# Unread TensorE products in the first stage's idle places, and the experts' ranks placed behind the one-hot tiles in the middle stage

## The chip, the cores and the metric

The kernel runs on one core of one Trainium2 chip. Times are device microseconds from the start to the end of one execution; a median is taken over three runs. The engines are TensorE (PE; its weight loads are listed as PEld), VectorE (DVE), ScalarE (ACT), GpSimd (POOL) and SyncE (SP). Each takes its own instructions in order; semaphores tie the engines together. SP issues most DMAs, POOL issues the ones that go through an index list.

## The reference

Attention over clusters, and on its output a mixture of eight experts of which each token uses two.

```python
mask = q_assign[:, :, :, None] == k_assign[:, :, None, :]
scores = scale * np.matmul(q, k.transpose(0, 1, 3, 2))
scores = np.where(mask, scores, -1000000000.0)
attn = np.exp(scores - max); attn = attn / (sum + 1e-09)
x = np.matmul(attn, v)                    # 4 x 768 tokens, 8 heads of 64 -> 3072 x 512
noisy_logits = x @ w_gate + np.log1p(np.exp(x @ w_noise)) * noise
top2 = np.argpartition(-noisy_logits, 2, axis=1)[:, :2]
h = np.maximum(x[mask] @ w1[e], 0.0)      # 512 -> 1024, for each expert e
out[mask] += top2_w[mask, k, None] * (h @ w2[e])
```

`q_assign` and `k_assign` are the nearest of 16 centroids. Batch 4, 8 heads, 768 positions, head size 64.

## The kernel before, in words

Attention runs over 16 pairs of heads, `p = 0..15`. For each pair 12 steps follow, one for each head of the pair and each block of 128 keys: `scores` multiplies keys with queries into two PSUM banks (`e0`, `e1`), ACT takes exp, POOL subtracts a bf16 half to leave a rest (`pl`), and `values` multiplies both halves with `v` into the bank `av`, four steps behind. Queries and keys stand in SBUF as f32 halves whose products are labelled f32 in the trace; the products with `v` and the transposes of one-hot rows (`identb`, `oh`, `gl`) are bf16 or f16. The largest score of each query is needed ahead of the exp: `b_max` (line 1049), for pair 0 `r_max` (line 1066), makes all scores once more and DVE reduces them (lines 1051, 1069). `r_max` works on half a block at a time; its products go to a ring of three banks, two for each half, and each is reduced from there.

A table of due steps (`AT`, `MOVE`) sets where in the loop each helper is issued. What stands ahead of step 0 is written out in the list `FIRST`: the load of the first queries, the clusters of pairs 0 and 1 (`a_sims`, line 952; `a_turn`, line 964; `a_max1`, `a_ge`, `a_ky`, `a_max2`, `a_eq` on DVE; `a_mask`, lines 1004 and 1015), and the first `r_max` calls. `b_negT` (line 1088) turns the largest scores.

Between attention and the experts lies the middle stage, whose order is the list `MID`: the gate of the last batch (`glog`, `glog2`, `gturn`, then `gate 0` to `gate 40`, where `gate 26` holds products on PE), the first layer of expert 0 on its first four tiles of tokens (`l1a 0..7`, line 1913, tile of F each, 512 columns), its second layer (`l2`, line 1954), the split of weights into two f16 halves (`spw1`, `spw2`, lines 1793 and 1795), and the loads of the next weights (`ldw1`, `ldw2`, lines 1870 and 1879). The list of expert 0's last tokens is made by `hot` (one-hot rows, DVE line 1408), `ent` (POOL lines 1418 and 1420), `lsum` (products on PE, line 1429) and `lend` (DVE line 1435, writes `idx`). With `idx` POOL gathers the rows of token tiles 4, 5, 6 (`gx 0 4..6`, line 1893), SP transposes them (`turn 0 4..6`, line 1904), and `l1b 0..7` runs the first layer on them. `rank 0` (DVE lines 1535 to 1541) orders experts 1 to 7 by load; SP reads its result `ids` into registers (line 1542), and only then can it issue `ldw1 1 0..3`, the four 512 KB loads of the next expert's `w1`. `rank 1` and `rank 2` (lines 1549, 1551) bring the lists into that order. All items of one engine keep the order of `MID`.

Of the kernel before, what the change touches and what calls it, by code (L numbers as in the profile page):

```python
# [9 lines left out]
F32 = mybir.dt.float32  # L10
# [24 lines left out]
    gate=7.667, gstep=[0.667, 0.167], am=5.333, amstep=0.333, cut=[13, 20], gplace=17.333,  # L35
# [244 lines left out]
}  # L280

FIRST = """fixed_init 1
c_turn
load_qk 0 0
a_hi 0 0
load_qk 0 1
a_sims 0
a_lo 0 0
constants2
load_qk 1  # L290
a_copy 0
a_turn 0
a_max1 0
a_ge 0
a_ky 0
# [16 lines left out]
r_max 0 1  # L312
r_max 0 0
a_turn 1
a_max1 1
p_hi 1 0
b_neg 0 0 1
# [13 lines left out]
a_max2 1""".splitlines()  # L331


MID = """turn 0 0
turn 0 1
turn 0 2
turn 0 3
gpg
spw1 0 0 1
spw1 0 1 1  # L340
spw1 0 2 1
spw1 0 3 1
ldw2 0 1
ldw2 0 2
ldw2 0 3
ldlist
mxw2 0 0
glog 0
glog 1
glog2 0  # L350
glog 2
glog2 1
glog 3
glog2 2
glog 4
glog2 3
glog 5
glog2 4
glog2 5
gturn  # L360
gate 0
gate 1
gate 2
gate 3
gate 4
# [5 lines left out]
gate 10  # L371
gate 11
gate 12
mxw2 0 1
l1a 0
xhi 13 0
xhi 13 1
xlo 13 0
xlo 13 1
xput 13  # L380
gate 13
gate 14
gate 15
gate 16
gate 17
gate 18
gate 19
l1a 1
xhi 14 0
xhi 14 1  # L390
xlo 14 0
xlo 14 1
xput 14
gate 20
gate 21
gate 22
gate 23
gate 24
gate 25
mxw2 0 2  # L400
l1a 2
xhi 15 0
xhi 15 1
xlo 15 0
xlo 15 1
xput 15
mxw2 0 3
l1a 3
gate 26
l1a 4  # L410
w2s 0 0
gate 27
gate 28
gate 29
gate 30
gate 31
l1a 5
w2s 0 1
gate 32
gate 33  # L420
gate 34
gate 35
spw2 0 0 0
spw2 0 0 1
l1a 6
spw2 0 1 0
spw2 0 1 1
l1a 7
spw2 0 2 0
spw2 0 2 1  # L430
spw2 0 3 0
spw2 0 3 1
eff 0 4
gate 36
gate 37
gate 38
gate 39
gate 40
l2 0
hot 0  # L440
ent 0 0
ent 0 1
hot 1
ent 1 0
ent 1 1
l2 1
lsum 0
lsum 1
lend 0
lend 1  # L450
eff 4 7
gx 0 4
gx 0 5
gx 0 6
rank 0
ldw1 1 0
ldw1 1 1
ldw1 1 2
ldw1 1 3
rank 1  # L460
rank 2
l2 2
count
mxw1 1 0
turn 0 4
turn 0 5
turn 0 6
gx 1 0
gx 1 1
gx 1 2  # L470
gx 1 3
l2 3
mxw1 1 1
mxw1 1 2
mxw1 1 3
l1b 0
l1b 1
w1s 1 0
l1b 2
w1s 1 1  # L480
turn 1 0
gx 1 4
l1b 3
turn 1 1
gx 1 5
l1b 4
ldw2 1 0
turn 1 2
gx 1 6
l1b 5  # L490
ldw2 1 1
mxw2 1 0
turn 1 3
l1b 6
ldw2 1 2
mxw2 1 1
l1b 7
pv
turn 1 4
l2 4  # L500
spw1 1 0 0
spw1 1 0 1
ldw2 1 3
mxw2 1 2
turn 1 5
turn 1 6
l2 5
spw1 1 1 0
spw1 1 1 1
spw1 1 2 0  # L510
spw1 1 2 1
spw1 1 3 0
spw1 1 3 1
mxw2 1 3
l2 6
ldcount""".splitlines()


def rap(tensor, offset, dims):
# [3 lines left out]
class Kernel:  # L523
# [128 lines left out]

    def psm(self):
        return self.bank("side")

    def rnorm(self, n, r):

        nc = self.nc
        nc.vector.tensor_scalar(n, n, 1e-37, None, op0=OP.max)
        nc.scalar.activation(r[:, 0:1], n, AF.Sqrt)  # L660
        nc.vector.reciprocal(r[:, 1:2], r[:, 0:1])
        nc.vector.scalar_tensor_tensor(n, n, r[:, 1:2], r[:, 0:1], op0=OP.mult, op1=OP.add)
        nc.vector.tensor_scalar(n, n, 0.5, 1e-6, op0=OP.mult, op1=OP.add)
        nc.vector.reciprocal(n, n)
# [23 lines left out]
    def attention(self, ctx):  # L688
        nc, tc = self.nc, self.tc
        B, H, S, D, NJ = self.B, self.H, self.S, self.D, self.NJ  # L690
# [132 lines left out]
        rank = {self.a_lo: -1, self.a_hi: 1}  # L823
        for t in range(min(sched)[0], z + L + 2):
            u = t - L
            slot = lambda i: [f(*a) for _, f, a in sorted(sched.pop((t, i), []), key=lambda x: x[0] + rank.get(x[1], 0) if t > -24 else 0)]
            slot(0)
            if 0 <= t < z:
                self.scores(t // 12, (t % 12) // 6, t % 6)
            if 0 <= t - 1 < z:  # L830
                self.split_p((t - 1) // 12, ((t - 1) % 12) // 6, (t - 1) % 6)
            slot(1)
            if 0 <= u < z:
                p, s, kc = u // 12, (u % 12) // 6, u % 6
                for i in range(NJ):
                    if AT["vd"][i] == kc:
                        self.values(p, s, i)
            slot(2)
        assert not sched

    def first(self, do):
        for f in FIRST:
            name, *a = f.split()
            by = [self.nc.scalar] if a[-1:] == ["ACT"] else []
            do(getattr(self, name), *(int(x) for x in a[:len(a) - len(by)]), *by)
# [207 lines left out]
    def r_max(self, p, j, half=None):  # L1053

        nc, st, NJ = self.nc, self.st[p], self.NJ
        hl, mk = st["hl"], st["mk"]
        if "mm" not in st:
            st["mm"] = self.wk.tile([128, 2 * NJ, 2], F32, name="mm")
        js = slice(j * 128, j * 128 + 128)
        for n in range(2) if half is None else (half,):  # L1060
            ns = slice(n * 384, n * 384 + 384)
            ts = [self.ps()[:, :384] for s in range(2)]
            for a, b, first in ((hl[:, 1], hl[:, 2], True), (mk[:, 0], mk[:, 1], False)):
                for s in range(2):
                    r = slice(64 * s, 64 * s + 64)
                    nc.tensor.matmul(ts[s], a[r, js], b[r, ns], start=first, stop=not first)
            for s in range(2):
                c = NJ * s + j if p else NJ * (j // 3) + 3 * s + j % 3
                nc.vector.tensor_reduce(st["mm"][:, c, n:n + 1], ts[s], axis=X, op=OP.max, negate=True)
# [65 lines left out]
    def values(self, p, s, kc):  # L1135
        nc, st, H, D, NJ = self.nc, self.st[p], self.H, self.D, self.NJ
        b, hp = divmod(p, H // 2)
        h = 2 * hp + s
        if kc == 0:
            st["av", s] = self.psum.tile([128, NJ, 65], F32, name="av", bufs=1)  # L1140
            if s == 0:
                if p < self.NP - 2:
                    self.xp[p] = self.gp.tile([128, NJ, 128], F32, name="xp", bufs=2)
                else:
                    t = self.mw.tile([128, self.F], F32, name="stg", bufs=7)
                    self.xp[p] = t[:, :NJ * 128].rearrange("p (j c) -> p j c", c=128)
        av = st["av", s]
        vv, am = self.vv[b, h // 4], self.am[b, h // 4]
        head = (lambda j: 2 * (hp % 2) + j // 3) if p in ROWS else (lambda j: h % 4)
        ph, pl = st.pop(("p", s, kc))  # L1150
        kj = 2 * (kc % 3) + kc // 3
        for j in range(NJ):
            js = slice(j * 128, j * 128 + 128)
            nc.tensor.matmul(av[:, j, :], ph[:, js], vv[:, head(j), kj, 64:129], start=(kc == 0 and j == 0),  # L1154
                             stop=False, skip_group_check=True)
            nc.tensor.matmul(av[:, j, :64], ph[:, js], vv[:, head(j), kj, 0:64], start=False,  # L1156
                             stop=False, skip_group_check=True)
        for j in range(NJ):
            js = slice(j * 128, j * 128 + 128)
            nc.tensor.matmul(av[:, j, :], pl[:, js], vv[:, head(j), kj, 64:129], start=False,  # L1160
                             stop=(kc == NJ - 1), skip_group_check=True)
        if kc == NJ - 1:
            rs = self.wk.tile([128, NJ], F32, name="rs")
            if p in ROWS:
                xo = self.xp[p].rearrange("p (m a) (s d) -> p a s m d", a=2, s=2)[:, s]
            else:
                xo = self.xp[p].rearrange("p (j a) c -> p a j c", a=2)[:, :, :, s * D:s * D + D]
            nc.vector.tensor_scalar(rs, av[:, :, 64], 64e-9, am[:, 0:1] if p else am[:, 2:3], op0=OP.add, op1=OP.mult)
            nc.vector.reciprocal(rs, rs)
            two = lambda x: x.rearrange("p (a j) d -> p a j d", a=2)  # L1170
            nc.vector.tensor_tensor(xo, two(av[:, :, 0:64]), two(rs[:, :, None].to_broadcast([128, NJ, D])), op=OP.mult)
# [424 lines left out]
    def experts(self, ctx):  # L1596
# [13 lines left out]
        self.fs = self.g_gate(b)  # L1610
        for item in MID:
            name, *a = item.split()
# [413 lines left out]
```

## Time and profile before

| what | us |
|---|---|
| median of 3 runs | 1004.48 (1002.84 to 1007.99) |
| the profiled execution, its own time | 1005.61 |
| its span, first to last instruction | 1003.8 |
| PE busy in it | 948.3 (94%) |
| DVE, POOL, ACT busy | 653.6, 565.9, 487.5 |
| mean granted TensorE clock | 0.976 |

A row of a timeline gives start, duration, engine, line, operation, output and inputs, how many instructions are merged in it, and in brackets the time that the engine stood idle ahead of it and what ended that. A row of a table by stretches gives busy time (and number of instructions) of each engine. The granted clock is a share of 2.4 GHz, so 0.50 is 1.2 GHz.

### The profile page before, as it was taken

Reading aid. Unit: us, or ns where it says so; the run is one execution under the profiler, and the core shown is the slowest. Engines: PE = TensorE matmul, PEld = TensorE weight load, DVE = VectorE, ACT = ScalarE, POOL = GpSimd, SP = SyncE. Lnnn points to the kernel's source line nnn. Section 1 sums busy time; section 2 is a strip of 40 time slices with the busy share of each in tenths; the row PEclk is TensorE's granted clock in tenths of the full one; section 3 lists DMA queues with packets and bytes.
Section 4 is the critical chain, followed back from the end, with each engine's and each line's share of the span. In section 5 each row is a group of like instructions: output and inputs, shape, how many; then the busy total and the mean of one; then the engine's idle time right before and its main releaser. Section 6 shows DMA issues by size and latency. Waiting matters only on the chain. (4 is left out here: it accounts for less than half of the span.)

```text
span 1003.8 us, 21267 instructions
## 1 busy us (share of the span) xinstructions
PE 948.3 (94%) x8063; PEld 609.8 (61%) x8063; DVE 653.6 (65%) x1406; ACT 487.5 (49%) x1081; POOL 565.9 (56%) x649
## 2 busy tenths in 40 slices
PE   5999999999989998789789999999999999999997
PEld 2567788887878887664455545445455455454553
DVE  6678788888878978856636555456555564565421
ACT  3567778786868684467042415306224153151420
POOL 9369898899999999912435225225243352342301
PEclk9599999999999999999989999999999999999999
DMA  5377999999989963071495925728529358294201
GB/s 176 94 174 187 207 239 208 241 207 246 209 195 215 220 138 109 11 163 49 154 196 148 247 98 127 231 87 210 184 68 263 117 120 231 81 233 142 81 11 51
DMA packets 146160, 159.72 MB, mean 159 GB/s; under 512 B 85213, under 2 KB 112093, under 8 KB 146054
## 3 DMA queue, kind: packets, MB, share of 16 engines
q1 hardware_dynamic: 132668, 120.95, 50.0%
q0 software_dynamic: 12864, 36.37, 11.6%
q10 hardware_dynamic: 522, 1.00, 0.5%
q8 instruction: 64, 1.05, 0.5%
q14 instruction: 42, 0.34, 0.1%
HBM read 77.30 MB, written 26.05 MB: 103 GB/s over the span
## 5 line engine op out<-in xcount | busy, mean ns | idle before, releaser
L1132 POOL TENSOR_TENSOR pl<-pe 128x768 f16<-128x768 f32 x173 | 250.9, 1467 | 28.2 <-ACT pe L1113 10.4
L1913 PEld LDWEIGHTS <-w1t 128*128 128x128 f16 x1536 | 149.9, 98 | 119.9 <-DMA xT<-xg 8.8
L1051 DVE TENSOR_REDUCE mm<-m 128x1 f32<-128x384 f32 x360 | 186.3, 550 | 24.5 <-PE m L1049 22.7
L1121 ACT ACTIVATE pe<-e 128x384 f32<-128x384 f32 x360 | 157.0, 489 | 90.0 <-PE e L1120 84.1
L1954 PEld LDWEIGHTS <-hT 128*128 128x128 f16 x1152 | 112.2, 98 | 133.9 <-issue 1.1
L1966 POOL DMA_INDIRECT out<-yo,idx x50 | 60.2, 1204 | 228.8 <-DVE yo L1962 103.3
L1913 PE MATMUL m<-xT,w1t 128*128 128x400 f16 (+4 forms) x756 | 163.0, 333 | 0.0
L1913 PE MATMUL e<-xT,w1t 128*128 128x400 f16 (+4 forms) x528 | 133.8, 338 | 8.6 <-DMA xT<-xg 8.0
L1119 PE MATMUL e<-A 128*128 128x384 f32 x360 | 131.4, 365 | 7.0 <-issue 2.7
L1789 DVE TENSOR_TENSOR hT<-hr,hT 128x384 f16<-128x384 f32 (+6 forms) x128 | 70.1, 557 | 88.0 <-ACT hT L1788 68.6
L1954 PE MATMUL m<-w2t,hT 128*128 128x512 f16 x576 | 127.0, 379 | 0.0
L1049 PE MATMUL m<-A 128*128 128x384 f32 x360 | 119.6, 382 | 5.7 <-DVE mm L1051 1.7
L1120 PE MATMUL e<-B 128*128 128x384 f32 x360 | 122.3, 340 | 0.0
L1154 PE MATMUL av<-vv,pe 128*128 128x65 f16 x1152 | 98.3, 196 | 0.0
L1156 PE MATMUL av<-vv,pe 128*128 128x64 f16 x1152 | 96.9, 193 | 0.0
L1893 POOL DMA_INDIRECT xg<-xs,idx x50 | 51.9, 1038 | 77.4 <-DMA xT<-xg 67.1
L1154 PEld LDWEIGHTS <-pe 128*128 128x128 bf16 x1152 | 76.7, 98 | 22.9 <-issue 18.7
L1786 ACT ACTIVATE hr<-m 128x400 f32<-128x400 f32 (+4 forms) x63 | 32.1, 509 | 117.1 <-PE m L1913 105.6
L1786 ACT ACTIVATE hr<-e 128x400 f32<-128x400 f32 (+4 forms) x44 | 22.5, 511 | 129.7 <-PE e L1913 92.3
L1954 PE MATMUL e<-w2t,hT 128*128 128x512 f16 x384 | 85.0, 379 | 0.0
L1049 PEld LDWEIGHTS m<-A 128*128 128x128 f32 x360 | 64.9, 192 | 24.8 <-DVE mm L1051 13.5
L1913 PE MATMUL side<-xT,w1t 128*128 128x400 f16 (+4 forms) x252 | 78.6, 334 | 0.0
(302 smaller groups left out, 1567.9 us busy)
## 6 DMA issues: line engine op xcount, KB each, us to landing
stg<-in_moe_w SPq DMA_DIRECT2D x64, 512.0 KB
qt<-in_qk SPq DMA_DIRECT2D x15, 768.0 KB
A<-hl SPq DMA_DIRECT2D x28, 384.0 KB
B<-hl SPq DMA_DIRECT2D x28, 384.0 KB
vt<-in_v SPq DMA_DIRECT2D x8, 768.0 KB
out<-zt SPq DMA_DIRECT2D x12, 512.0 KB
xs<-xh SPq DMA_DIRECT2D x15, 384.0 KB
A<-hl SPq DMA_DIRECT2D x56, 96.0 KB
```

The source lines that it names most:

```text
L1049: nc.tensor.matmul(t, A[:, s, 0, j * 128:j * 128 + 128], A[:, s, 1, n * 384:n * 384 + 384], start=True, stop=True)
L1051: nc.vector.tensor_reduce(st["mm"][:, self.NJ * s + j, n:n + 1], t, axis=X, op=OP.max, negate=True)
L1119: nc.tensor.matmul(t, A[:, s, 1, ks], A[:, s, 0, ns], start=True, stop=False)
L1120: nc.tensor.matmul(t, Bt[:, 0, s, ks], Bt[:, 1, s, ns], start=False, stop=True)
L1121: nc.scalar.activation(pe[:, n], t, AF.Exp, scale=self.scale)
L1132: (nc.vector if last else nc.gpsimd).tensor_tensor(lo, pe, hi, op=OP.subtract)
L1154: nc.tensor.matmul(av[:, j, :], ph[:, js], vv[:, head(j), kj, 64:129], start=(kc == 0 and j == 0), stop=False, skip_group_check=True)
L1156: nc.tensor.matmul(av[:, j, :64], ph[:, js], vv[:, head(j), kj, 0:64], start=False, stop=False, skip_group_check=True)
L1789: nc.vector.tensor_tensor(h1, r[:, a:b], h0, op=OP.subtract)
L1913: nc.tensor.matmul(p, self.w1t[:, wi, c, f * 128:f * 128 + 128], self.xT[e][:, c, xi, n0:n1], start=(i == 0), stop=(i == 3 * ND - 1))
L1954: nc.tensor.matmul(p, self.hT[:, hi, f, t * 128:t * 128 + 128], self.w2t[:, wi, f], start=(i == 0), stop=(i == 3 * NF - 1))
L1966: i = nc.gpsimd.indirect_dma_start(out=self.out, out_offset=bass.IndirectOffsetOnAxis(ap=en[:r], axis=0), in_=yo[:r], in_offset=None, boun ...
```

## The change

Two things are changed. The list `FIRST` and the function `r_max` get groups of products of the bf16 identity with itself, written to bank `e1`, which nothing reads: 10, 2, 2, 18 and 4 in `FIRST` and 2 in each half of `r_max` for blocks 0 to 4 (20), each 384 columns wide. In steps 11 and 12 eight more, 122 columns wide, go to the unused end of bank `av`, whose tile is now a whole bank. And the order of `MID` is rewritten.

```diff
 FIRST = """fixed_init 1
+warm 10
 c_turn
+warm 2
 load_qk 0 0
...
 a_lo 0 0
+warm 2
 constants2
...
 a_turn 0
+warm 18
 a_max1 0
...
 a_turn 1
+warm 4
 a_max1 1
...
+    def warm(self, n):
+        t = self.bank("e1")
+        for _ in range(n):
+            self.nc.tensor.matmul(t[:, :384], self.identb, self.identb[:, None, :].to_broadcast([128, 3, 128]), start=True, stop=True)
+    def warm_av(self, n):
+        for _ in range(n):
+            self.nc.tensor.matmul(self.avt[:, 390:512], self.identb, self.identb[:, :122], start=False, stop=False,
+                                  skip_group_check=True)
...
+            if t in (11, 12):
+                self.warm_av(8)
             if 0 <= t < z:
                 self.scores(t // 12, (t % 12) // 6, t % 6)
...
+            if j < NJ - 1:
+                self.warm(2)
             for s in range(2):
...
-            st["av", s] = self.psum.tile([128, NJ, 65], F32, name="av", bufs=1)
+            self.avt = self.bank("av")
+            st["av", s] = self.avt[:, :65 * NJ].rearrange("p (j c) -> p j c", c=65)
```

Of `MID`, the part after `l1a 3` now reads

```diff
+l1a 3
+gate 38
+gate 39
+hot 0
+mxw2 0 3
+xput 14
+hot 1
...
+rank 0
+ldw1 1 2
+ldw1 1 0
...
 l1a 7
+lsum 0
...
 lsum 1
 lend 0
```

The four rows of `r_max` products for one half are followed on PE at once by the next half's in the kernel before (output, then inputs; the number after a name tells buffers apart):

```order
L1066 MATMUL m_258<-A_117 128x384
L1066 MATMUL m_259<-A_117 128x384
L1066 MATMUL m_258<-B_120 128x384
L1066 MATMUL m_259<-B_120 128x384
L1066 MATMUL m_268<-A_117 128x384
L1066 MATMUL m_269<-A_117 128x384
L1066 MATMUL m_268<-B_120 128x384
L1066 MATMUL m_269<-B_120 128x384
```

and now, with the line numbers of the changed kernel:

```order
L1085 MATMUL m_297<-A_117 128x384
L1085 MATMUL m_298<-A_117 128x384
L1085 MATMUL m_297<-B_120 128x384
L1085 MATMUL m_298<-B_120 128x384
L665 LDWEIGHTS identb
L665 MATMUL e_303<-identb 128x384
L665 LDWEIGHTS identb
L665 MATMUL e_303<-identb 128x384
L1085 MATMUL m_310<-A_117 128x384
L1085 MATMUL m_311<-A_117 128x384
```

Two weight loads and two products on bank `e1` stand between the halves. In the middle stage DVE's order from the one-hot tiles to the ranks was, before:

```order
L1408 TENSOR_TENSOR hot<-aux,lower 128x768 x2
L1960 TENSOR_SCALAR yo<-m_9459,we 128x512
L1435 TENSOR_TENSOR idx<-m_9490,lst 128x56
L1437 TENSOR_TENSOR lsw<-m_9490,lst 128x56
L1862 TENSOR_SCALAR we<-lsw,ce 128x3
L1535 SCALAR_TENSOR_TENSOR rk<-base,num 128x8
L1536 TENSOR_TENSOR rg<-rk 128x49
L1537 TENSOR_REDUCE rk<-rg 128x7
L1538 TENSOR_TENSOR perm<-rk,num 128x49
L1539 TENSOR_TENSOR rg<-perm,num 128x49
L1541 TENSOR_REDUCE ids<-rg 128x7
```

and is now (`hT` is the rest half of a tile of the first layer):

```order
L1811 TENSOR_TENSOR hT<-hr,hT 128x512
L1409 TENSOR_TENSOR pk<-aux,pk 128x12
L1410 SCALAR_TENSOR_TENSOR rec<-aux,px,gm 128x6
L1430 TENSOR_TENSOR hot<-aux,lower 128x768 x2
L1811 TENSOR_TENSOR hT<-hr,hT 128x512
L1395 TENSOR_TENSOR base<-aux,base 128x8
L1829 TENSOR_REDUCE gmax<-m_9434 4x1
L1830 TENSOR_SCALAR gmax<-gmax 4x1
L1557 SCALAR_TENSOR_TENSOR rk<-base,num 128x8
L1558 TENSOR_TENSOR rg<-rk 128x49
L1559 TENSOR_REDUCE rk<-rg 128x7
```

The ranks no longer stand behind the second layer's output `yo` and the list `idx`; they follow the one-hot tiles with one `hT` between, and the one-hot tiles follow the fourth `hT` and not the eighth. On PE the products of `lsum` stood between the second and the third output tile of the second layer (line 1954 and 1976):

```order
L1954 LDWEIGHTS hT
L1954 MATMUL m_9459<-w2t,hT 128x512
L1429 MATMUL m_9490<-ent,hot 128x112 x12
L1954 LDWEIGHTS hT
L1954 MATMUL m_9563<-w2t,hT 128x512
```

Now they stand between the last hidden tile and the first output tile:

```order
L1935 LDWEIGHTS w1t
L1935 MATMUL e_9530<-xT,w1t 128x512
L1451 MATMUL side<-ent,hot 128x112 x12
L1976 LDWEIGHTS hT
L1976 MATMUL m_9586<-w2t,hT 128x512
```

The two output tiles that were ahead of `lsum` are behind it. In all PE has 144 rows more, a weight load and a product for each of the 72 unread products.

## Rows read from the trace of the kernel before

**Rows 1.** Busy time by stretches (from:to, length, each engine, granted clock, DMA share, GB/s)
```profile
0.00:17.00 17.00, 6.13 (x34) 2.63 (x36) 9.46 (x32) 7.46 (x13) 15.84 (x39) 1.00 0.41 148
17.00:20.50 3.50, 2.64 (x15) 1.46 (x14) 2.88 (x6) 0.34 (x1) 3.33 (x6) 0.99 0.96 264
20.50:31.20 10.70, 8.37 (x30) 5.13 (x30) 9.17 (x21) 1.55 (x2) 4.99 (x7) 0.50 0.65 142
31.20:51.20 20.00, 19.32 (x87) 12.57 (x85) 11.65 (x27) 12.01 (x26) 9.08 (x8) 0.50 0.32 90
...
450.40:496.60 46.20, 45.65 (x236) 22.17 (x234) 30.12 (x85) 19.23 (x37) 16.48 (x25) 1.00 0.27 80
496.60:504.60 8.00, 0.00 (x1) 0.00 (x0) 4.32 (x4) 0.00 (x0) 1.11 (x2) 0.82 0.97 270
504.60:520.80 16.20, 15.53 (x99) 10.42 (x100) 5.73 (x21) 5.80 (x21) 7.87 (x8) 0.88 1.06 221
```
**Rows 2.** Timeline of PE in the first stage
```profile
6.59 1.51 PE L952 MATMUL side<-qt,cb 128*32 128x384 f32 x8 [0.63 <-DVE cb L686]
8.71 0.90 PE L964 MATMUL side<-ident,sm 128*128 128x128 f32 x3 [0.61 <-ACT sm L958]
13.50 0.82 PE L1004 MATMUL side<-identb,gl 128*128 128x128 bf16 x6 [3.88 <-DVE gl L988]
...
15.22 1.51 PE L952 MATMUL side<-qt,cb 128*32 128x384 f32 x8 [0.26 <-ACT B L1009]
...
25.97 0.45 PE L1088 MATMUL m<-ident,nm 128*128 128x128 f32 x1 [1.29 <-DVE nm L1083]
```
**Rows 3.** Timeline of PE, the same operations later, at granted clock 1.00
```profile
55.16 0.49 PE L964 MATMUL side<-ident,sm 128*128 128x128 f32 x3
64.52 0.51 PE L1015 MATMUL side<-identb,oh 128*128 128x128 bf16 x6 [0.67 <-DVE oh L993]
70.79 0.85 PE L952 MATMUL side<-qt,cb 128*32 128x384 f32 x8
```
**Rows 4.** Timeline of DVE in the first stage
```profile
1.28 0.86 DVE L555 TENSOR_SCALAR identb<-lg 128x128 bf16<-128x128 f32 x1
12.88 0.56 DVE L988 TENSOR_TENSOR gl<-side,km 128x384 bf16<-128x384 f32 x1 [0.73 <-POOL gl L858]
17.47 3.22 DVE L1069 TENSOR_REDUCE mm<-m 128x1 f32<-128x384 f32 x6 [1.85 <-PE m L1066]
20.89 1.02 DVE L1069 TENSOR_REDUCE mm<-m 128x1 f32<-128x384 f32 x2 [0.19 <-PE m L1066]
22.23 1.02 DVE L1069 TENSOR_REDUCE mm<-m 128x1 f32<-128x384 f32 x2 [0.32 <-PE m L1066]
```
**Rows 5.** Timeline of PE after the middle stage's idle time
```profile
504.65 3.36 PE L1913 MATMUL e<-xT,w1t 128*128 128x320 f16 x12 [8.04 <-DMA xT<-xg]
507.80 2.17 PE L1913 MATMUL side<-xT,w1t 128*128 128x320 f16 x12
...
509.92 1.79 PE L1913 MATMUL m<-xT,w1t 128*128 128x320 f16 x12
512.33 0.38 PE L1814 MATMUL m<-gmax,fw 4*128 4x1 f32 x2 [0.62 <-DVE gmax L1808]
```
**Rows 6.** Timeline of SP's DMA issues
```profile
491.02 2.02 SPq L1870 DMA_DIRECT2D stg<-in_moe_w  x4
493.16 15.59 SPq L1904 DMA_TRANSPOSE xT<-xg  x5
```
**Rows 7.** Timelines of POOL and DVE around the lists of expert 0
```profile
486.77 1.04 POOL L1893 DMA_INDIRECT xg<-xs,idx  x1 [1.10 <-DVE lsw L1437]
...
487.99 0.20 DVE L1541 TENSOR_REDUCE ids<-rg 128x7 int32<-128x49 f32 x1
```
**Rows 8.** Timeline of PE in the middle stage
```profile
467.00 5.35 PE L1913 MATMUL e<-xT,w1t 128*128 128x512 f16 x24
...
483.74 2.51 PE L1429 MATMUL m<-ent,hot 128*128 128x112 f32 x21
```

More of the change, by code (lines that the diff above doesn't have):

```diff
@@ L331 @@
 a_max2 1""".splitlines()
-MID = """turn 0 0
+MID = """gpg
+spw1 0 0 1
+mxw2 0 0
+spw1 0 1 1
+turn 0 0
 turn 0 1
@@ L337 @@
 turn 0 3
[L338 to L341, printed above, removed]
+glog 0
+ldw2 0 1
+ldw2 0 3
 spw1 0 3 1
[L343 to L348, printed above, removed]
 glog 1
+glog 2
 glog2 0
-glog 2
 glog2 1
 glog 3
+spw1 0 2 1
 glog2 2
 glog 4
+glog 5
 glog2 3
-glog 5
 glog2 4
+ldlist
 glog2 5
@@ L362 @@
 gate 1
+ldw2 0 2
+xhi 13 0
 gate 2
@@ L373 @@
 gate 12
[L374 to L377, printed above, removed]
+gate 13
 xlo 13 0
-xlo 13 1
-xput 13
-gate 13
 gate 14
@@ L387 @@
 gate 19
-l1a 1
+gate 20
+gate 22
+gate 23
+gate 34
+gate 24
+gate 25
+l1a 2
+mxw2 0 1
+xhi 13 1
 xhi 14 0
 xhi 14 1
+gate 21
+l1a 0
+xlo 13 1
+l1a 1
+mxw2 0 2
 xlo 14 0
+gate 26
+gate 28
 xlo 14 1
[L393 to L401, printed above, removed]
-xhi 15 0
[L403 to L414, printed above, removed]
+xput 13
+xhi 15 0
 gate 30
 gate 31
+xhi 15 1
+gate 33
+gate 37
+gate 27
+xlo 15 0
+gate 36
+xlo 15 1
+gate 40
+gate 32
+gate 35
+l1a 3
[5 more added lines that the diff above has]
+hot 1
+ent 0 0
+xput 15
+l1a 4
+gate 29
+w2s 0 0
+ent 1 0
+rank 0
+ldw1 1 2
+ldw1 1 0
+ent 1 1
 l1a 5
+ent 0 1
+ldw1 1 1
+ldw1 1 3
 w2s 0 1
[L419 to L422, printed above, removed]
 spw2 0 0 0
@@ L426 @@
 spw2 0 1 0
-spw2 0 1 1
 l1a 7
+lsum 0
 spw2 0 2 0
[L430 to L447, printed above, removed]
 lsum 1
 lend 0
-lend 1
-eff 4 7
+spw2 0 3 0
 gx 0 4
 gx 0 5
-gx 0 6
[L455 to L459, printed above, removed]
-rank 1
[L461 to L467, printed above, removed]
+turn 0 4
+eff 0 4
+spw2 0 1 1
+turn 0 5
+lend 1
+gx 0 6
+turn 0 6
+spw2 0 2 1
+spw2 0 3 1
+mxw1 1 0
+l2 0
+l2 1
+mxw1 1 1
+mxw1 1 3
+mxw1 1 2
+l2 2
+w1s 1 0
+rank 2
+rank 1
+gx 1 1
 gx 1 0
-gx 1 1
+gx 1 4
 gx 1 2
-gx 1 3
-l2 3
-mxw1 1 1
-mxw1 1 2
-mxw1 1 3
+eff 4 7
+ldw2 1 1
+l2 3
+w1s 1 1
+ldw2 1 0
+mxw2 1 0
+turn 1 0
+gx 1 5
 l1b 0
 l1b 1
-w1s 1 0
 l1b 2
-w1s 1 1
-turn 1 0
-gx 1 4
 l1b 3
+gx 1 6
+l1b 4
+l1b 5
 turn 1 1
-gx 1 5
-l1b 4
-ldw2 1 0
+l1b 6
 turn 1 2
[L489 to L496, printed above, removed]
 l1b 7
-pv
-turn 1 4
-l2 4
 spw1 1 0 0
 spw1 1 0 1
-ldw2 1 3
-mxw2 1 2
-turn 1 5
[L506 to L514, printed above, removed]
-l2 6
-ldcount""".splitlines()
+spw1 1 2 0
+spw1 1 3 0
+spw1 1 1 0
+spw1 1 2 1
+spw1 1 1 1
+count
+ldw2 1 2
+gx 1 3
+spw1 1 3 1
+mxw2 1 2
+l2 4
+ldw2 1 3
+turn 1 3
+mxw2 1 1
+l2 5
+pv
+mxw2 1 3
+turn 1 4
+turn 1 5
+l2 6
+ldcount
+turn 1 6""".splitlines()
 def rap(tensor, offset, dims):
```

## The prediction, made before the changed kernel ran

> **What bounds the kernel now.** I read the table of stretches first [rows 1]: it tells in which stages PE is not the whole of the time, and at which of its two levels the clock stands there. From 450 us on PE is busy nearly throughout, but for one hole: 8.00 us from 496.6 with no product. In the first stage it is idle 10.9 of the first 17 us, and from 20.5 to 51.2 it works at 0.50, that is 1.2 GHz; from 31.2 it is busy 19.32 of 20.00 us and still at 0.50. Next I read PE's timeline there [rows 2]. The table says clock 1.00 for the first 17 us, but the durations say otherwise: three transposes take 0.90 us at 8.71 and 0.49 us later, six one-hot transposes 0.82 against 0.51, the eight sims products 1.51 against 0.85 [rows 2, 3]. I take the durations: half clock up to about 16.7 us, full to 20.5, half again to 51.2. Third, DVE's timeline [rows 4]: the reduces of the first six run back to back (3.22 us for six); with the clock down, each pair of them waits for PE. Last the hole [rows 5 to 7]: PE waits for the transposes of expert 0's last three token tiles, SP issues them at 493.16 behind four loads of `w1` (491.02), those wait for `ids` (487.99), and the gather itself starts at 486.77.
>
> So two places can give time: the half clock of the first stage, and the hole with the slow products behind it. Elsewhere PE's own work is the time, and the change leaves it alone.
>
> **The first stage, part by part.** A product of 384 columns is not in the trace. Twelve of 320 take 3.36 us at half clock and 1.79 at full [rows 5]; by columns that makes 0.32 us and 0.16 us (an estimate from these rows). The 72 added products are 56 of these, 9 us at full clock or 18 at half, and 16 of 122 columns, under 1 us.
>
> The first 10 can start when `identb` is there, at 2.14 us [rows 4], and take 3.2 us at half clock: done at 5.4, when ScalarE's centroids come (the sims products follow at 6.59). The next two pairs lie in gaps of 0.63 and 0.61 us [rows 2], which they fill: cost 0 to 0.1 us each. The 18 behind the transposes at 8.71 lie in a gap of 3.88 us [rows 2]: 2.9 us at full clock, hidden, 5.8 at half, of which 1.9 stick out. I take full clock, since in the trace a burst of transposes and sims products from 13.50 to 16.7 was followed by it, and here 3 us of products and the sims stand ahead.
>
> Gain at the start: DVE's `gl` cannot be earlier, it waits for POOL (12.88) [rows 4]. Behind it the two times six transposes and the sims products shrink by 0.31 and 0.66 us on the path, some 1.1 us with ScalarE between; bounds 0 and 1.3.
>
> Gain in `r_max`: DVE is busy 9.17 of 10.70 us there [rows 1]. Its waits of 0.19 and four times 0.32 us [rows 4] go at full clock: 1.5 us. The two products added for each half take 0.33 us, in the time in which PE waits for DVE's reduce (a pair of reduces is 1.02 us, PE's four products some 0.5). Cost 0 at full clock. At half clock they take 0.64 us of a half that PE already sets; ten halves then lose some 0.3 us each, 3 us. The group of 4 lies in a gap of 1.29 us [rows 2].
>
> Then the scores, 20.00 us at half clock [rows 1], from step 0 to the first product with `v`. No unread products stand there. Will the clock hold? Before it fell at 20.5, PE had done only f32 products since 16.7; and 19 us of f32 products on a busy PE did not bring it back [rows 1]. In contrast the f16 products at 504.65 were at full clock after 3.2 us [rows 5]. So in this kernel f32 products do not seem to hold it. The last bf16 product is the one-hot transposes behind step 0; I let the full clock last some 4 us past them, as it did from 16.7. Some 5 us of work at full clock replace 7 at half: 2 us. Later the products with `v` begin at half clock, which costs 0.5 us that before did not. First stage: 1.1 + 1.5 + 2 - 0.5 = 4.1 us.
>
> If the clock held throughout, the 20 us would shrink to about 14 (ScalarE alone has 12.01 us of work there, DVE 11.65 [rows 1]): 1.1 + 1.5 + 6 = 8.6 us, less what waits anew; say 8. The rest of attention follows in the same order and PE-bound, so what is gained by then stays.
>
> The Trainium skill ("TensorE: Matmul & The Clock Gate", section "Why this matters for your kernels") asks only for a TensorE kept busy without long gaps to have the full clock. By that rule the unread products hold it and the busy scores keep it: 8 us instead of 4.1. The rows speak against it: busy 19.32 of 20.00 us, clock 0.50 [rows 1]. The same page (section "Terms") puts the loss at the throttled time times one minus the clock's share. By that, 30.7 us at half would give back 15.4 us. The rows put ScalarE and DVE in the way, 12.01 and 11.65 us in the 20, 9.17 in the 10.7 [rows 1]; I keep 4.1.
>
> **The middle stage.** Now `lsum` follows the last hidden tile, which ended at 467.00 + 5.35 = 472.3 us [rows 8]. Its one-hot tiles and entries must be there by then. PE's place products come after three hidden tiles instead of four; behind them DVE has the small gate operations, one `hT` and the two one-hot tiles, about 6 us, and POOL's eight entries end some 2 us later: about 468, an estimate with 4 us to spare. So `lsum` ends at 472.3 + 2.5 = 474.8, and `idx` is there 11.5 us before its present place: the gather moves from 486.77 to about 475.3 [rows 7]. The `ids` come about 469 instead of 487.99, and the four loads about 472 instead of 491 [rows 6]. Those loads lie beside expert 0's first and second layers, in a stretch with a DMA share of 0.27 [rows 1]. The three transposes then land before 490, while PE's work for `l2 0..3` still ends near 496.6: its sum is unchanged, `lsum` only moves. The hole of 8.04 us goes [rows 5].
>
> With no hole the clock does not fall: the first twelve products of `l1b` take 1.79 instead of 3.36 us, the next 1.79 instead of 2.17, and the wait of 0.62 for `gmax` goes, because the scale of the next `w1` stands ahead of `l1b` now [rows 5]. Together 8.04 + 1.57 + 0.38 + 0.62 = 10.6 us.
>
> What is late next: expert 1's inputs. Its first product would come at about 523. Its seven gathers and transposes start when `rank 1` is done, behind the third output tile: 474.8 + 3 x 5.2 = 490.4 [rows 8], and some 4 us of DVE work, say 495. Five transposes took 15.59 us beside loads [rows 6], 3.1 us each; seven take 22, and two loads of `w2` (the four of `w1` held the queue some 9 us, so 2.3 each) another 4.6. That is 26.4 of 28 us. The last transposes also stand behind the register load of the overflow count. I take 0.7 us of loss; bounds 0 and 6 (4 us for each transpose, with share 1.06 [rows 1]).
>
> The sum against the profiled execution's own 1005.61 us: 4.1 + 10.6 - 0.7 = 14.0, so 991.6. That execution stands 1.1 us above the median of 1004.48; against the median 990.5.
>
> **Rivals.** A: the clock holds through the first stage (for it: the rule above; against: the rows named there): 8 + 10 = 18 us, 986.5. B: the unread products do not hold the clock in `r_max`, being a minority beside f32 work. Then 1.1 us are gained at the start and the 3 us of the ten halves lost; with 9.9 us of the middle stage, about 996. That the products change nothing in the clock at all belongs here. C: the hole is only moved to expert 1's start: 4.1 + 10.6 - 6 leaves 8.7, so 996. D, slower: the 56 products run at half clock and none is hidden, 18 us, because they sit ahead of the operations that PE is waited for. It decides from 34 of the 56 exposed (10.6 us): 1004.48 + 18 - 10.6 = 1012. Against it: gaps of 0.61 to 3.88 us are measured at most places.
>
> **How the numbers follow.** Forecast 0.48 (its own range 988 to 993.5), A 0.18, B 0.15, C 0.13, D 0.06. The unknown costs (start 0 to 1.3, the unread products in `r_max` 0 to 3, expert 1 0 to 6) take the range to 984.5 below, into A, and 998 above, over B and C. Half a per cent is 5 us, about what this kernel's measurement can tell from no change (three runs spread over 5.15 us). Above 999.5 lie the tail of B and C with both losses (0.06) and D: faster 0.89, same 0.06, slower 0.05.
>
> **What would show it.** Full clock from about 7 us, one-hot transposes in 0.5 us, `r_max` reduces without waits, clock falling again some 5 us into the scores (not at all: A; before `r_max`: B). In the middle: loads of `w1` issued near 472, `lsum` right behind the hidden tiles, no wait for `xT` ahead of `l1b`, its first twelve products in 1.8 us, expert 1 starting near 523 less the first stage's gain. A PE wait there for `xT` is C. I am wrong if the end of `l2 3` is late, because the hidden tiles wait for DVE's gate operations ahead of them.

## The result, and the profile after

| | us, median | runs |
|---|---|---|
| before | 1004.7 (1000.4 to 1017.9) | 18 |
| after | 992.39 (990.3 to 1001.0) | 18 |
| ratio | 0.9874, 95% interval 0.9855 to 0.9893 | |
| forecast | 990.5 (984.5 to 998.0) | |

The change brings 12.7 us (1004.7 x 0.0126; by the interval 10.8 to 14.6). The forecast had 14.0. The profiled execution took 992.97 us, its span 991.2.

Kernels are compared only with the kernel before on the same chip, since the chips differ: its medians there were 1004.7, 1007.5 and 996.5, and single runs took 994.4 and 996.0 us. In one execution each of two kernels the time was 5317 us, and the one profile of these shows TensorE at a sixth of its rate (24 products of 512 columns take 32.09 us, in the changed kernel 5.34); they enter no median or ratio of this text, and the repeat of the changed kernel below has no other profile.

The table of stretches of the changed kernel, in the form of [rows 1] (length, busy time of PE, PEld, DVE, ACT and POOL, granted clock, DMA share, GB/s). The first three are stretches of [rows 1], the fourth is the part of them at half clock, the last three are the middle stage: hidden tiles with `lsum`, output tiles 0 to 3, `l1b`.

```profile
0.00:17.00 17.00, 11.65 (x73) 5.39 (x73) 10.10 (x34) 7.80 (x13) 15.84 (x39) 1.00 0.41 145
20.50:31.20 10.70, 9.65 (x59) 4.94 (x56) 10.15 (x23) 2.15 (x4) 4.98 (x7) 1.00 0.84 176
31.20:51.20 20.00, 18.08 (x146) 12.49 (x148) 13.77 (x32) 12.47 (x28) 12.05 (x10) 0.83 0.44 112
36.18:43.01 6.83, 6.50 (x25) 4.58 (x25) 3.75 (x11) 4.21 (x11) 3.79 (x3) 0.50 0.16 47
447.64:473.38 25.74, 24.56 (x139) 12.71 (x138) 19.88 (x61) 18.49 (x37) 10.13 (x15) 1.00 0.35 109
473.38:494.61 21.23, 21.23 (x101) 9.65 (x100) 13.97 (x21) 0.75 (x1) 9.06 (x11) 1.00 0.67 187
494.61:507.66 13.05, 13.05 (x97) 9.41 (x97) 5.89 (x19) 5.80 (x21) 6.90 (x8) 1.00 0.92 225
```

`r_max` now runs at 1.00, the scores at 0.50 only from 36.18 to 43.01, and in the middle stage the stretch without a product is gone.

PE's timeline of the first stage, to be read against [rows 2 and 3]:

```profile
2.19 3.38 PE L665 MATMUL e<-identb 128*128 128x384 bf16 x10 [2.19 <-DVE identb L560]
...
6.45 0.85 PE L971 MATMUL side<-qt,cb 128*32 128x384 f32 x8 [0.30 <-DVE cb L703]
...
8.30 3.09 PE L665 MATMUL e<-identb 128*128 128x384 bf16 x18
13.49 0.51 PE L1023 MATMUL side<-identb,gl 128*128 128x128 bf16 x6 [2.10 <-DVE gl L1007]
...
29.59 0.93 PE L1132 MATMUL e<-A 64*128 64x384 f32 x6
...
36.52 1.30 PE L1068 MATMUL m<-A 128*128 128x384 f32 x3 [0.86 <-DVE am L923]
...
45.79 0.20 PE L1176 MATMUL av<-vv,pe 128*128 128x65 f16 x1
```

The first ten unread products take 0.34 us each, half clock. The sims products behind them already take 0.85 instead of 1.51, and the one-hot transposes 0.51 instead of 0.82. The first product with `v` stands at 45.79; before it was at 51.23:

```profile
51.23 0.21 PE L1154 MATMUL av<-vv,pe 128*128 128x65 f16 x1
```

VectorE's timeline there, against [rows 4]: the first reduces, and the first maximum of `v` behind them; then the same maximum before.

```profile
16.34 6.60 DVE L1090 TENSOR_REDUCE mm<-m 128x1 f32<-128x384 f32 x12 [0.74 <-PE m L1085]
...
30.05 1.80 DVE L903 TENSOR_REDUCE vq<-vt 128x1 f32<-128x768 f32 x2
```
```profile
32.42 1.80 DVE L884 TENSOR_REDUCE vq<-vt 128x1 f32<-128x768 f32 x2
```

Twelve reduces in a row without a wait; before, five of the seven pairs from 20.89 on had one. The start is 1.13 us earlier (17.47 to 16.34).

PE's timeline of the middle stage, against [rows 5 and 8]:

```profile
462.42 0.27 PE L1827 MATMUL m<-ident,wm 128*4 128x128 f32 x1 [1.18 <-ACT w2t L1864]
...
470.72 2.83 PE L1451 MATMUL side<-ent,hot 128*128 128x112 f32 x24
473.38 15.70 PE L1976 MATMUL m<-w2t,hT 128*128 128x512 f16 x72
...
494.61 5.06 PE L1935 MATMUL m<-xT,w1t 128*128 128x320 f16 x36
...
520.83 0.35 PE L1935 MATMUL side<-xT,w1t 128*128 128x416 f16 x1
```

The last row is expert 1's first product. Before, the first hidden tile, the first output tile and expert 1's first product stood at

```profile
450.59 5.34 PE L1913 MATMUL m<-xT,w1t 128*128 128x512 f16 x24
...
472.19 1.89 PE L1954 MATMUL side<-w2t,hT 128*128 128x512 f16 x8
...
533.97 0.35 PE L1913 MATMUL side<-xT,w1t 128*128 128x416 f16 x1
```

The timelines of SP, POOL and DVE there, against [rows 6 and 7]:

```profile
469.08 2.13 SPq L1892 DMA_DIRECT2D stg<-in_moe_w  x4
478.93 4.84 SPq L1926 DMA_TRANSPOSE xT<-xg  x3
```
```profile
474.07 1.98 POOL L1915 DMA_INDIRECT xg<-xs,idx  x1 [8.92 <-DVE we L1884]
...
466.19 0.20 DVE L1563 TENSOR_REDUCE ids<-rg 128x7 int32<-128x49 f32 x1
```

`l1b` starts without a wait, the transposes having been issued 15.7 us ahead of it. The stage itself begins 2.95 us earlier, so in the time of before these stand at 472.0 (loads), 477.0 (gather) and 469.1 (`ids`); forecast were 472, 475.3 and 469.

### The profile page after: what moved, and what is told of

Its sections match the earlier page's. It is cut to its first block, busy times and chain, and to the rows that moved or that the text cites. A ratio compares the mean times of both kernels' runs of the same rounds, so it can differ in the third digit from the quotient of the medians.

```text
span 991.2 us, 21414 instructions
## 1 busy us (share of the span) xinstructions
PE 947.8 (96%) x8135; PEld 609.6 (62%) x8135; DVE 655.8 (66%) x1406; ACT 487.7 (49%) x1081; POOL 568.9 (57%) x649
## 5 line engine op out<-in xcount | busy, mean ns | idle before, releaser
L1935 PE MATMUL m<-xT,w1t 128*128 128x400 f16 (+4 forms) x780 | 166.3, 332 | 0.0
L1976 PE MATMUL m<-w2t,hT 128*128 128x512 f16 x600 | 132.2, 379 | 1.0 <-DVE hT L1811 1.0
L1935 PE MATMUL e<-xT,w1t 128*128 128x400 f16 (+4 forms) x516 | 130.5, 335 | 0.0
L1176 PEld LDWEIGHTS <-pe 128*128 128x128 bf16 x1152 | 77.0, 98 | 22.9 <-issue 18.4
L1140 PEld LDWEIGHTS e<-A 128*128 128x128 f32 x360 | 69.3, 193 | 15.6 <-ACT pe L1142 9.2
L1178 PEld LDWEIGHTS <-pe 128*128 128x128 bf16 x1152 | 78.8, 99 | 0.1
```

The costliest lines, as they stand in the source:

```text
L1140: nc.tensor.matmul(t, A[:, s, 1, ks], A[:, s, 0, ns], start=True, stop=False)
L1935: nc.tensor.matmul(p, self.w1t[:, wi, c, f * 128:f * 128 + 128], self.xT[e][:, c, xi, n0:n1], start=(i == 0), stop=(i == 3 * ND - 1))
L1976: nc.tensor.matmul(p, self.hT[:, hi, f, t * 128:t * 128 + 128], self.w2t[:, wi, f], start=(i == 0), stop=(i == 3 * NF - 1))
```

## The experiments

What each profile showed, in us. Half clock is where the record shows 0.50, up to 55 us, and, ahead of the record's first entry, where the durations are those of half clock (the table of stretches prints 1.00 there, see the end); the middle stage is from its first hidden tile to expert 1's first product. The kernels above the line have the old first stage, those in the middle the new one without a further change, the rest a varied one.

| kernel | half clock | first scores | first `v` | first hidden tile | middle stage |
|---|---|---|---|---|---|
| before | to 51.2 but for 17.0 to 20.5 | 31.24 | 51.23 | 450.59 | 83.38 |
| before, again | to 36.7, 40.1 to 50.4 | 32.08 | 50.81 | 442.00 | 83.17 |
| new middle list only | to 36.6, 40.0 to 43.5 | 32.09 | 48.16 | 450.81 | 73.19 |
| --- | | | | | |
| after | to 5.5, 36.2 to 43.0 | 29.59 | 45.79 | 447.64 | 73.19 |
| unread products only | to 7.9 | 29.61 | 44.36 | 446.60 | 82.99 |
| loads' place in the list | to 6.0, 26.5 to 33.3 | 30.91 | 46.42 | 438.18 | 73.51 |
| sums late | to 8.1, 14.9 to 18.3, 38.8 to 49.1 | 30.99 | 48.82 | 440.77 | 74.61 |
| 64 more in the last steps | to 7.8 | 29.61 | 44.34 | 441.41 | 73.19 |
| --- | | | | | |
| without those in `r_max` | to 5.8, 19.5 to 26.3, 29.7 to 33.1 | 29.53 | 44.98 | 450.84 | 73.18 |
| `r_max` only | to 18.9, 39.4 to 49.6 | 31.41 | 49.33 | 451.12 | 73.19 |
| f32 in `r_max` | to 6.0, 36.7 to 43.5 | 30.05 | 46.21 | 438.68 | 73.18 |
| 13 more in the scores | to 5.2, 15.5 to 18.9 | 30.78 | 46.69 | 437.90 | 73.19 |
| both additions | to 6.2, 26.7 to 30.1 | 30.51 | 46.40 | 443.41 | 73.18 |

**The two halves of the change, on one chip.** The unread products with the old middle list (left), and the new middle list alone (right), both in short:

```
-MID = (the new list)        -warm, warm_av and their calls
+MID = (the old list)        (the old MID stays out)
```

> The changed kernel with the middle stage's old list, so only the unread products are new. Theory: the lead of 5.4 us at the first product with v (51.23 to about 45.8) comes from them alone; attention gives back 2 to 3 us of it before the middle stage, whose idle place of 8 us is back. Some 1001.5 us, 3 less than before. Rival (the lead is lost whole in attention, because POOL, DMA or DVE bound it there): 1004. Rival (the lead is kept whole, and what the changed kernel lost at 48, 128 and 415 us is chance): 999.

> The kernel before with the new list of the middle stage and no unread product. Theory: no product waits for xT at expert 0's last three tiles, and no fall of the clock at 501; from the middle stage's first hidden tile to expert 1's first product 73.2 us instead of 83.4: 994 us. First product with v at 51.2 as before. Rival (part of the middle gain needs the unread products, because the stage was entered with another clock): 998 or more.

Ratios to the kernel before: unread products 0.9937 (0.9900 to 0.9973), that is 6.3 us (2.7 to 10.1) of 1007.5; middle list 0.9886 (0.9837 to 0.9936), 11.5 us (6.4 to 16.4). Both halves gain alone. The middle stage takes 73.19 us with the new list and 82.99 without it, as expected. Between the two the lead at the first `v` is 3.80 us and at the first hidden tile 4.21: nothing is given back in between, against my expectation. In neither was the first stage's clock that of the pair predicted from: half clock ended at 36.6 with the instructions for which before showed 51.2, and did not return at all in the other.

**Parts of the unread products**, on the same chip:

```
-            if j < NJ - 1:
-                self.warm(2)
```
```
-warm 10 (and the other five warm lines of FIRST)
```

> The changed kernel without the unread products between the r_max halves; those of the first 8 us and the 4 behind step 1's transposes stay. Theory: full clock from 5.5 us as in the changed kernel, but with r_max's f32 products alone it falls before the scores, somewhere between 16 and 24 us, and the first product with v comes 2 to 4 us later than 45.8, at 48 to 50: 994 to 996 us. Rival (the products in r_max do nothing for the clock, the first 8 us alone set it): first v at 45.8 or earlier, 992.

> The changed kernel without the unread products of the first stage's list (36 of 56); the 20 between the r_max halves stay. Theory: half clock up to 16.7 us as before, so 1.1 us later at r_max; from there full clock through r_max, and the first product with v at about 47: 993 to 994 us. Rival (without the early ones the unread products of r_max meet a clock that falls at 20 us as before, and cost time instead of bringing it): first v at 51 to 54, 997 to 999 us.

Ratios 0.9882 (0.9818 to 0.9947) and 0.9853 (0.9810 to 0.9896): the intervals hold the middle list's 0.9886, so the times decide nothing about the parts. Each has one profile: without the products in `r_max` the first `v` came at 44.98, where 48 to 50 was expected, though the clock did fall there as expected; with them alone at 49.33, not 47. That points to the early products and gives no sign of a gain by those in `r_max`. But five profiles of the full first stage spread from 44.3 to 48.8, so one profile each does not show it.

**Before once more.**

> The kernel before once more, one look. In the kernel with only the new middle list, whose first stage has the same instructions as before, the clock rose at 36.6 us, not at 51.2, and the first product with v came at 48.2. Theory: where the clock rises and falls differs from execution to execution of the same instructions, so this look shows the half clock of the first stage ending elsewhere than at 51.2, and the first product with v somewhere between 47 and 52; the middle stage, from its first hidden tile to expert 1's first product, takes 83.0 to 83.4 us again. Rival (the times of the clock belong to the instructions): half clock from 20.5 to 51.2, first v at 51.2.

995.97 us beside 994.35 for the same kernel. Half clock to 36.7 and from 40.1 to 50.4, first `v` at 50.81: the times of the clock differ between executions of the same instructions. The middle stage does not (83.17).

**f32 instead of bf16 in `r_max`.**

```
-                self.warm(2)
+                tw = self.bank("e1")[:, :384]
+                for _ in range(2):
+                    nc.tensor.matmul(tw, hl[:, 1, js], hl[:, 2, ns], start=True, stop=True)
```

> The changed kernel with the 20 unread products of r_max in f32 (two heads' rows of hl by hl, 384 columns) instead of bf16. By the step of the prediction that f32 products do not hold the clock, it falls inside r_max or before step 2 of the scores, and the first product with v comes at 48 to 51. Rival (a busy TensorE holds it whatever the type): full clock through r_max as with bf16, first v at 45 to 46.5. Middle stage 73.2 us.

The table of stretches of this kernel, `r_max` and then the scores:

```profile
15.70:30.00 14.30, 13.38 (x72) 7.67 (x68) 12.60 (x28) 2.04 (x3) 9.61 (x12) 1.00 0.79 180
30.05:46.21 16.16, 14.35 (x85) 9.43 (x85) 10.92 (x25) 11.08 (x25) 8.54 (x8) 0.79 0.40 112
```

With these 20 in f32 the clock stays at 1.00 (the group of 4 behind step 1's transposes is still bf16), and the first `v` comes at 46.21: in this one execution the rival holds. 982.73 us, one run, beside 994.35 for the kernel before.

**Which move closed the middle stage's hole.** The loads of `w1` back behind the gather in the list (with the first of their maxima behind the second output tile); and `lsum`, gather and transposes behind the second output tile (the lists in short):

```
-rank 0 / ldw1 1 2 / ldw1 1 0 / ... / ldw1 1 1 / ldw1 1 3
+rank 0 / ...     gx 0 5 / ldw1 1 2 / 1 0 / 1 1 / 1 3 / turn 0 4
```
```
-l1a 7 / lsum 0 / lsum 1 / lend 0 / gx 0 4..6 / turn 0 4..6 / l2 0 / l2 1
+l1a 7 / l2 0 / l2 1 / lsum 0 / lsum 1 / lend 0 / gx 0 4..6 / turn 0 4..6
```

> The changed kernel with the four loads of expert 1's w1 ahead of the three transposes again (and the first of their maxima behind the second output tile, so that VectorE does not wait for it). The lists and the gather stay early. Theory (the early gather alone closes the hole): the transposes are issued near 484 instead of 479, land before 494.6, and the middle stage takes 73 to 74 us. Rival (the queue behind the loads was the cause of the hole): PE waits for xT before l1b, 3 to 6 us, 76 to 80 us.

> The changed kernel with the sums of expert 0's list, the gather and its transposes behind the second output tile again, some 10.4 us later; the loads of w1 stay early. Theory: gather at 484.5 instead of 474.1, transposes at 489, and these take 5 to 9 us to land, against 494.6 when l1b needs them: a wait of 0 to 3 us, middle stage 73.2 to 77 us. Rival (the place of the sums is the whole cause): the hole of 8 us is back with the slow products behind it, 82 us.

The first missed its aim. SP's timeline:

```profile
459.62 2.13 SPq L1892 DMA_DIRECT2D stg<-in_moe_w  x4
469.41 4.82 SPq L1926 DMA_TRANSPOSE xT<-xg  x3
```

SP has nothing between them in either list, so it issues the loads as soon as `ids` is there, and they stay 9.8 us ahead of the transposes. Stage 73.51 us, one run 982.60: it says nothing about late loads. The second, SP and then PE:

```profile
462.22 2.13 SPq L1892 DMA_DIRECT2D stg<-in_moe_w  x4
482.25 4.63 SPq L1926 DMA_TRANSPOSE xT<-xg  x3
```
```profile
466.27 4.00 PE L1976 MATMUL side<-w2t,hT 128*128 128x512 f16 x16 [0.54 <-ACT w2t L1815]
...
489.17 5.05 PE L1935 MATMUL m<-xT,w1t 128*128 128x320 f16 x36 [0.28 <-DMA xT<-xg]
```

With `lsum` late again the wait for `xT` is 0.28 us, not 8.04, and the stage 74.61: transposes issued 20 us behind the loads are there in under 7 us, where before, 2.1 us behind them, they took 11.5 (493.16 to 504.65). Counted from the stage's first product, they land 5.7 us earlier than before; the other 2.1 us of the wait are gone because PE itself comes to `l1b` later in the new list. So all but 1.4 us of the stage's gain is there without the early sums. That the place of the loads is what did it is argued from these landings: the run that was to have them late did not, the rest of the new list is in both runs, and the early `lsum` alone was not tried.

**Three kernels on one chip: after again, and more unread products.** 13 of 384 columns at score steps 1 to 3; 64 of 122 columns ahead of steps 183, 184 and 187; both.

```
+            if t in (1, 2, 3):
+                self.warm_s(SW[0][t - 1])
             if 0 <= t < z:
                 self.scores(t // 12, (t % 12) // 6, t % 6)
+                if t in (1, 2, 3):
+                    self.warm_s(SW[1][t - 1])
```
```
-            if t in (11, 12):
-                self.warm_av(8)
+            if t in (11, 12, 183, 184, 187):
+                self.warm_av({183: 16, 184: 24, 187: 24}.get(t, 8))
```

> The changed kernel once more, beside the next three. Theory (the times of the clock differ between executions of the same instructions, and the unread products only shift the odds): first product with v between 44.4 and 48.8, the span of the four looks at this first stage so far (45.8, 44.4, 46.4, 48.8), the fall of the clock somewhere between 15 and 49 us; middle stage 73.2 us; ratio to before 0.985 to 0.99. Rival (45.8 belongs to the instructions): 45.8 and a fall at 36.2 again.

> The changed kernel with 13 more unread products of 384 columns in the waits of score steps 1 to 3, where PE stood still for 0.5 to 0.9 us before the clock fell. Theory (the clock falls there because PE stands still, whatever the type of its products): no fall between 33 and 50 us, first product with v at 43.5 to 44.5, as in the one look at this first stage that had no fall (44.4); some 1 to 2 us less than the changed kernel on the same chip. Rival (a clock that f32 products can't hold): the fall stays, first v at 46 to 48, no gain or 1 us of loss.

> The changed kernel with 64 more unread products of 122 columns ahead of score steps 183, 184 and 187, where PE stood still for 0.96, 1.87 and 2.11 us and the clock fell twice between 418 and 432 us. Theory (those falls give back the first stage's lead): where such stalls are, no fall there, the middle stage begins 1.5 to 3 us earlier: 990 for 992.4. On a chip without the stalls (three looks had none) the products stand in nobody's wait: 2 to 3 us more. Rival (the lead is lost in the stalls themselves, not in the clock): the middle stage begins no earlier with the clock held.

> The changed kernel with both additions. Theory: the sum of the two: 2.5 to 5 us less than the changed kernel where the stalls near 418 and 428 us are, 0 to 1 us more where they are not. Rival (both lost behind other waits): equal to the changed kernel within 1 us.

| kernel | us, median | ratio to before (996.45) |
|---|---|---|
| after, again | 981.3 | 0.9864 (0.9835 to 0.9893) |
| 13 in the scores | 983.3 | 0.9873 (0.9852 to 0.9895) |
| 64 in the last steps | 988.2 | 0.9920 (0.9896 to 0.9943) |
| both | 986.7 | 0.9904 (0.9882 to 0.9927) |

The changed kernel's ratio is repeated, with 13.6 us (10.7 to 16.4); its first `v` can't be read. The scores of the kernel with 13 more, and of the one with 64 more, which has no more there:

```profile
30.78:46.69 15.91, 14.48 (x98) 8.54 (x98) 10.96 (x26) 10.72 (x25) 8.26 (x8) 1.00 0.38 108
```
```profile
29.61:44.34 14.73, 12.11 (x86) 7.62 (x85) 11.04 (x26) 10.72 (x25) 8.26 (x8) 1.00 0.46 123
```

Both have the full clock. There was no fall in the scores, as the theory of the standstill has it; but the second had none either, so this does not bear the theory out, and its scores are 1.2 us shorter. The first `v` came at 46.69, not at 43.5 to 44.5. The fall that the 13 were to prevent costs about 1.5 us (16.20 in after against 14.73), so they bring next to nothing. In the last steps (PE of the kernel with 64 more):

```profile
413.18 1.02 PE L670 MATMUL av<-identb 128*128 128x122 bf16 x16
...
416.74 1.44 PE L670 MATMUL av<-identb 128*128 128x122 bf16 x24 [1.13 <-DVE stg L1193]
...
422.47 1.45 PE L670 MATMUL av<-identb 128*128 128x122 bf16 x24
```

3.91 us of products that nothing hides, as this chip has no stalls there, and 1.13 us in which they wait for VectorE's `stg`: 5.0 us. From the scores just ahead of them to the first hidden tile this kernel takes 34.21 us (407.20 to 441.41), the one with both 34.22, the one with the 13 alone 29.58 (408.32 to 437.90): the 64 cost 4.6 us, more than the 2 to 3 expected. The medians put it at 6.9 beside after and 3.4 beside the kernel with the 13. The kernel with both lies 5.4 us above after, where 0 to 1 was expected. The 64 were not run on a chip with the stalls, so whether such products help there is open. No version was shown to be faster than the changed kernel.

## Why the prediction was right

**The price of an unread product.** [rows 5] scaled by columns give 0.34 us at half clock and 0.18 at full, not the 0.32 and 0.16 of the prediction; measured are 0.34 (3.38 for ten) and 0.17 (3.09 for 18). It changes no choice between the rivals.

**The start: 1.1 us forecast, 1.13 measured** on VectorE's first reduce. The unread products had the clock up by 5.5 us in the record, before the 7 that I named (5.2 to 8.1 in the other profiles with the first list).

**`r_max`: 1.5 forecast.** The first maximum of `v` moved from 32.42 to 30.05, 2.37 us, of which 1.13 are the start: 1.24. The waits went as named; the reduces are a little longer (0.55 us a piece, 6.60 for 12, against 0.54). The term rests on a clock that holds through `r_max`, and it held in three of the seven profiles that have the whole first list and these products unchanged (those with the first `v` at 45.79, 44.36 and 44.34). In the other four there is half clock in it (falls at 26.5, 14.9, 15.5 and 26.7), and the scores began at 30.51 to 30.99 instead of 29.6.

**The scores: 1.5 forecast (2 less 0.5), 3.07 measured** (5.44 at the first `v`, less 2.37). This step failed: "So in this kernel f32 products do not seem to hold it." The clock fell at 36.2, 6.6 us into the scores instead of some 5, but returned at 43.0 amid f32 products. With f32 unread products `r_max` held it too, and in two executions it held through all the scores, which then took 14.75 and 14.73 us; rival A had "about 14". What the row I argued from showed, 19 busy us at 0.50, was one execution (with six bf16 transposes in it, 0.82 us at 32.97). The same instructions had 14.9 us at half clock within the scores in another (32.08 to 36.7 and 40.1 to 50.4) and 8.0 in a third.

The Trainium skill ("TensorE: Matmul & The Clock Gate", section "Why this matters for your kernels") has a TensorE without long gaps at the full clock. Those two executions agree with it; the repeat of before, busy 10.20 of 10.30 us at 0.50, does not:

```profile
40.10:50.40 10.30, 10.20 (x43) 5.64 (x41) 6.08 (x14) 7.39 (x19) 6.05 (x5) 0.50 0.09 23
```

So the size of the first stage's gain is a matter of odds. The five profiles of the new one put the first `v` at 44.3 to 48.8, mean 45.95; the three at the old one at 48.2 to 51.2, mean 50.07. The difference, 4.1 us, is the forecast's sum, and that is luck: the term for the scores was argued from the slowest of three executions, by a step that failed, and in the pair of profiles the stage gained 5.44.

**The middle stage: 10.6 less 0.7 forecast, 10.19 measured** (83.38 to 73.19), the same to 0.4 us in every profile but that with late sums. By parts: the hole 8.04, as forecast; `l1b` 3.10 (16.15 to 13.05) where 1.57 + 0.38 + 0.62 = 2.57 stood, and 0.42 of the rest are small products for the next `w1`'s scale that have moved among the output tiles; the output tiles 0 to 3 gain 0.53 with these added (from 472.19 to 504.65 less 8.04 and 2.66 of `lsum` are 21.76, now 21.23): a wait of 0.54 for `w2t` in the first of them, still there in the run with late sums, is gone; the hidden tiles lose 1.48 (21.60 to 23.08), of which 1.18 is the wait at 462.42, for ScalarE's `w2t` and not for the gate operations on VectorE that I had feared there. Expert 1 starts without a wait (rival C: none; I had 0.7). That the hole goes because lists and loads both come earlier was the reason given; the run with late sums shows that the early lists are worth 1.4 us; the rest is put down to the loads by the landings alone.

**Behind the stages.** In the two profiles of before and after the lead of 5.44 shrinks to 2.95 by the first hidden tile, and my sum had it stay. On one chip it stays: from the first `v` to the first hidden tile 402.65 and 402.24 us, on another 391.2 with the old first stage and 391.8 and 392.0 with the new. So the loss in the first pair does not repeat; its cause was not found.

**The sum.** 4.1 + 10.2 = 14.3 lies in both measured intervals (10.8 to 14.6, and 10.7 to 16.4), and in that of the two halves run alone (6.3 + 11.5 = 17.8, each within about 4 or 5). D did not come, the unread products were hidden; of B there is the half clock in `r_max` in four of seven profiles, but it took 0.9 to 1.4 us there, not the 3 of the rival.

## What to carry to other kernels

Read a stage whose time hangs on the clock in several executions before arguing from one: here the middle stage repeated to 0.4 us and the first stage moved by 4.5. Where a wait stands behind a queue, try first to bring forward what fills the queue: here the chain behind it could then stay late for 1.4 us. Put unread products only into a wait that is there on every chip: 64 of them in a stall of some chips cost 4.6 us on one without it.

## What the runs showed of the hardware that was not expected

The granted clock of the same instructions fell and rose at other times in each execution: before had 0.50 up to 51.2 in one, and up to 36.7 and from 40.1 to 50.4 in another. In the changed kernel's scores PE waits 0.48, 0.49 and 0.86 us before the fall at 36.18; in the kernel with 64 more, whose products there are the same, it waits 0.48, 0.48 and 0.85 us and the clock stays at 1.00. So neither these waits nor the type of the products decides it alone. What decides it stays open.

Ahead of its first entry the record is silent, and the table of stretches prints 1.00. Of the repeat of before, that table and PE's timeline:

```profile
20.00:30.00 10.00, 7.78 (x28) 4.64 (x26) 8.07 (x19) 0.45 (x2) 5.42 (x8) 1.00 0.56 121
```
```profile
24.62 0.90 PE L964 MATMUL side<-ident,sm 128*128 128x128 f32 x3
```

The three transposes take the 0.90 us of half clock there; at full clock they take 0.49 [rows 3]. Durations are to be read beside the clock.

Chips differ by 8 to 10 us in attention, nearly all of it between 410 and 440 us. The table of stretches from 400 to 440 us, of the changed kernel and, on another chip, of the one with the loads' place changed:

```profile
400.00:440.00 40.00, 31.93 (x463) 27.02 (x460) 26.82 (x42) 19.71 (x41) 24.93 (x32) 0.87 0.33 68
```
```profile
400.00:440.00 40.00, 35.72 (x558) 28.76 (x558) 33.68 (x54) 26.55 (x58) 25.60 (x33) 1.00 0.46 107
```

In the first PE and ACT stand still at times, with a releaser that the profile doesn't name (the changed kernel's timelines), and the clock falls:

```profile
419.59 0.69 PE L1140 MATMUL e<-A 128*128 128x384 f32 x1 [1.87 <-issue]
```
```profile
428.28 0.87 ACT L1142 ACTIVATE pe<-e 128x384 f32<-128x384 f32 x2 [3.39 <-remote]
```

The two profiles of the first pair and all four on the chip with 1007.5 us for before have such falls between 417 and 436, the seven on two other chips (994 to 997 us) none. What the engines wait for there was not found.
